# Set-attention and SwiGLU in one kernel: eight PSUM banks in one set, and one order for all steps behind the first gate product

## The chip, the cores and the metric

The kernel runs on one core of a Trainium2 chip, in one launch. The metric is the device time of one execution in microseconds (us). The engines are named as the profile names them: PE multiplies matrices (PEld is its weight load), DVE, ACT and POOL work element by element, and SP issues transfers. PSUM is the memory that PE writes its products to; it has eight banks, each of 128 x 512 numbers of four bytes.

## The reference

Four batches of 12416 tokens with 128 channels pass through attention with 32 inducing points, and then all 49664 tokens go through a normalised feed-forward part with 1536 inner columns.

```python
def mab(q, kv):
    s = scale * (q @ kv.transpose(0, 2, 1))
    s = s - s.max(-1, keepdims=True)
    a = np.exp(s)
    a /= a.sum(-1, keepdims=True) + 1e-09
    return a @ kv
h = mab(I, x)                  # 32 inducing points look at 12416 tokens
x = mab(x, h)                  # each token looks at the 32 points

rms = np.sqrt(np.mean(x * x, axis=-1, keepdims=True) + 1e-06)
xn = x / rms * rms_g
g = xn @ w_gate                # 128 -> 1536
silu = g * (1.0 / (1.0 + np.exp(-g)))
val = xn @ w_val               # 128 -> 1536
return (silu * val @ w_out).astype(np.float32)   # 1536 -> 128
```

## The kernel before

**Units and blocks.** A batch is cut into 25 units: 20 of 512 tokens, 4 of 480, and 1 of 256. The 1536 inner columns are cut into 12 groups of 128. A unit with one group is a block, so there are 100 units and 1200 blocks.

**One block.** PE makes the gate product (L682) from the unit's stacked attention weights, a tile `a` that holds an upper and a lower half, and a stacked factor matrix. ACT makes silu of it (L692); for a few blocks ACT makes tanh (L689) and DVE finishes the silu (L702). PE makes the value product (L710). DVE multiplies the two (L724, or L722 behind a tanh). The result must be multiplied by the 128 rows of w_out (`wo`) that belong to the block, and there are two ways to do it:

- A *plain* block (kind P) multiplies in full float32 (L781 from `wo`, two instructions, each of half the tokens).
- A *split* block cuts the result and the weights into upper and lower parts that PE multiplies at its faster fp32r setting. ACT makes the upper part (L737 for kind S, out of PSUM; L734 for kind D, out of a factor tile). For kind S DVE makes the lower part (L743); for kind D POOL does (L750), and ACT scales the upper part down (L756). Then PE makes two products (`project_two`, L769 and L770) into a bank `ups`, POOL adds the two parts (`add_in_place`, L789), and PE makes the third product (L781 too, from `xn` or `more`) into the bank `acc`.

**One unit.** When the products into `ups` are done, ACT takes them into an output tile (`take_upper`, step E, L822). When those into `acc` are done, DVE adds `acc` to it (`finish`, step F, L834) and transposes it (`turn_out`, step T, L842), and SP stores it with four transfers (`store`, step O, L855). SP also gathers the tile `a` of each unit (L592) and loads x for the next batch by channels (L147).

**Around it.** Attention for the next batch, its softmax, the normalisation, and the stacking of the factor matrices (`stack_of`, L504) run between the blocks of the batch before. In the first batch three more pieces do: the weights of gate and value arrive as raw words and are rounded in chunks (`rounding`: power, upper, sign, lower, with the last multiplication on POOL, L286; `put`, L228, writes the chunk back, and L216 fetches the next raw words), and `wo` is split into its upper, lower and difference parts (`split_wo`, L609 to L621, and `last_of`, L631 to L639).

**What sets the order.** The function `first` writes out the work up to the first gate product. The first 26 blocks, all plain, follow a plan written by hand (`early`: a block number with each side step, and a string `prefix` that places their plain products). From block 26 on, a string `program` gives the order: one letter is one step (`g` gate, `s` silu, `v` value, `m` the product of both, `h` upper part, `l` and `n` lower part, `e` scaling, `q` project_two, `d` add, `r` third product, `p` plain product, `E` `F` `T` `O` the steps of a unit, `a` a gather, and a dot for the next side step, whose number stands in `taken`). The string `sorts` gives the kind of each block; `banks`, `holders` and `workers` give the names of PSUM banks, factor tiles and work tiles that the steps use, one after the other. The engines run their own instructions in the order in which they were issued; a step waits for its operands and for its tile to come free.

**PSUM and tiles.** The eight banks are divided: five by name for gate and value products and the side work, `gv0` to `gv4`; two in rotation for `acc`; and one for `ups`, with these lines:

```python
ps_gv = pool("ps_gv", 1, space=PSUM)
ps_acc = pool("ps_acc", 2, space=PSUM)
ps_u = pool("ps_u", 1, space=PSUM)
...
def bank():
    ...
    return ps_gv.tile([P, 512], F32, name="gv", tag=f"gv{n}")
```

Output tiles are two in rotation. Factor tiles are `u0` to `u8` and ten places in three rings that hold other data at first.

Of the kernel before, what the change touches and what calls it, by code (L numbers as in the profile page):

```python
# [23 lines left out]
def kernel(  # L24
# [10 lines left out]

# [47 lines left out]
    outp = pool("outp", 2)  # L117
    ps_gv = pool("ps_gv", 1, space=PSUM)
    ps_acc = pool("ps_acc", 2, space=PSUM)
    ps_u = pool("ps_u", 1, space=PSUM)  # L120
# [66 lines left out]
    def warm(n):  # L187
        ps = ps_acc.tile([P, 512], F32, name="acc")
        for _ in range(n):
            nc.tensor.matmul(ps[:, 0:P], ident[:], ident[:], start=True, stop=True)  # L190

    warm(7)
    ps = ps_gv.tile([P, 512], F32, name="gv", tag="gv4")
# [25 lines left out]
    w0 = {}  # L219

    def rounding(i, c):
# [4 lines left out]
        def put():  # L226
            if i < 2:
                nc.sync.dma_start(out=w32[i][c][:], in_=st["dst"])  # L228
            if unread:
                fetch_raw(*unread.pop(0))  # L230
# [11 lines left out]
        def power():  # L242
            if i < 2:
                t = (xnp.tile([P, 512], F32, name=f"xn{2 * c - 1 + i}") if c else
                     silp.tile([P, 512], F32, name="silu") if i else halves.tile([P, 512], F32, name="lo"))
                w0[i, c] = t[:]
                dst = st["dst"] = w0[i, c]
            else:
                dst = st["dst"] = wo.rearrange("p j c -> p (j c)")[:, ts(c, 512)]
# [16 lines left out]
        def upper():  # L266
            if wide:
                f = st["f"] = outp.tile([P, 512], I32, name="o")
# [12 lines left out]
        def lower():  # L281
            if wide:
                e, f = st["e"], st["f"].bitcast(F32)
                nc.vector.scalar_tensor_tensor(out=f[:], in0=st["low"].bitcast(U32), scalar=2.0 ** -52, in1=f[:],
                                               op0=ALU.mult, op1=ALU.add)
                nc.gpsimd.tensor_tensor(out=st["dst"], in0=f[:], in1=e.bitcast(F32)[:], op=ALU.mult)  # L286
            put()
# [6 lines left out]
    NB, turn, turns, works, factors = 5, [0], [], [int(c) for c in "01201212"], []  # L294

    def bank():
# [5 lines left out]
        return ps_gv.tile([P, 512], F32, name="gv", tag=f"gv{n}")  # L302
# [5 lines left out]
    def attention(b, load_next):  # L308
# [192 lines left out]
        def stack_of(i, c):  # L501
# [3 lines left out]
            nc.scalar.copy(out=stacks[b][i][:, ts(c, 512)], in_=ps[:])  # L505
# [78 lines left out]
    def gather(b, u):  # L584
# [4 lines left out]
        a = moving[b, u] = (xnp.tile([P, 512], F32R, name="xn0") if (b, u) == (0, 2) else  # L589
# [4 lines left out]
    def split_wo(step):  # L594

        if not step:
            kws["first"] = xnp.tile([P, half + NK, C], F32R, name=f"xn{full - 1}")
            rings = [xnp.tile([P, RING * 512], F32R, name=f"xn{full - 4 + n}") for n in range(3)]
            kws["room"] = [ring[:, ts(n, 512)] for ring in rings for n in range(RING)][:3 * RING - 2]
            kws["wide"], kws["own"] = rings[2], {}  # L600

        def part(kind, g):
            n = kind * NK + g * half
            t = kws["first"][:, n:n + half, :] if n < half + NK else kws["more"][:, n - half - NK:n - NK, :]
            return t, t.bitcast(F32)

        def scaled(kind, g, mul, src=None):
            to, now = part(kind, g)
            nc.scalar.activation(to, now if src is None else src, AF.Copy, scale=mul)  # L609

        for g in range(2):
            one = wo[:, g * half:(g + 1) * half, :]
            at = step - g
            if at == 0:
                scaled(0, g, 1.0 - 2.0 ** -13, one)
            if at == 1:
                nc.gpsimd.tensor_tensor(out=part(1, g)[0], in0=one, in1=part(0, g)[1], op=ALU.subtract)
            if at == 3:
                scaled(1, g, 4096.0)
            if at == 4:  # L620
                nc.gpsimd.tensor_tensor(out=part(2, g)[0], in0=part(0, g)[1], in1=part(1, g)[1], op=ALU.subtract)  # L621
            if at == 6:
                scaled(0, g, -4096.0)

    def last_of(step):

        n = NJ - NK
        room = rings_last()
        one, (whi, wlo, ws) = wo[:, NK:NJ, :], (room[:, ts(kind, n), :] for kind in range(3))
# [11 lines left out]
    def rings_last():  # L641
        return kws["wide"][:, 2 * 512:4 * 512].rearrange("p (k c) -> p k c", c=C)

    def weight_of(kind, j):
        if j >= NK:
            return rings_last()[:, kind * (NJ - NK) + j - NK, :]
        n = kind * NK + j
        return kws["first"][:, n, :] if n < half + NK else kws["more"][:, n - half - NK, :]

    blocks, kinds = [], []  # L650
    at_unit = {}
    lists = {name: [] for name in "hlneqdDrRpx"}
# [3 lines left out]
    def unit_of(b, u):  # L656
        if (b, u) not in at_unit:
            s, q = units[u]
            at_unit[b, u] = {"T": per2[s] * m, "a": moving.pop((b, u)), "left": NJ, "q": 0, "acc": None,
                             "k": sum(kind != "P" for kind, one in zip(kinds, blocks) if one[:2] == (b, u)), "ups": None,  # L660
                             "o": None}
# [6 lines left out]
    def factor():  # L668
        return up.tile([P, 512], F32, name="u", tag=f"u{factors.pop(0)}")

    def room():
        n = factors.pop(0)
        if n < HELD and n not in kws["own"]:
            kws["own"][n] = up.tile([P, 512], F32R, name="u", tag=f"u{n}")[:]
        return kws["own"][n] if n < HELD else kws["room"][n - HELD]
# [36 lines left out]
    def times_value():  # L712
# [5 lines left out]
        else:  # L718
            factor_of[n] = {"u": factor()[:, 0:T]}
# [39 lines left out]
    def project_two():  # L759
# [5 lines left out]
        if one["ups"] is None:  # L765
# [724 lines left out]
```

## Time and profile before

| | |
|---|---|
| median of 3 runs | 1512.47 us (1512.46 to 1514.63) |
| profiled execution, span | 1513.0 us |
| first gate product | 47.3 us |
| last gate product | 1502.6 us |
| PE busy | 1496.2 us, 7138 matmuls |
| DVE busy | 1454.9 us, 2570 instructions |
| POOL busy | 1362.4 us, 1114 instructions |
| ACT busy | 1268.6 us, 2457 instructions |

The profile is of one execution, and its span is the time that the page gives for it; it lies 0.5 us above the median of the runs. Busy time of PE runs past the point at which the next matmul can start, so the distance between two starts tells more than the duration of a record. In the list of groups, a line of a helper stands for all its callers: L781 holds the plain products (out of `wo`) and the third products of split blocks (out of `xn` and `more`). In the blocks counted from the kernel, 384 are plain and 816 are split (657 of kind S, 159 of kind D).

### The profile page before, as it was taken

The numbers are of one execution on the slowest core, as the hardware profiler recorded it, in microseconds if no ns is written. First come the engines' busy times: TensorE is split into PE (matmuls) and PEld (weight loads), VectorE is DVE, ScalarE is ACT, GpSimd is POOL, SyncE is SP. The second block draws the span as 40 slices with busy tenths as digits, with TensorE's granted clock in tenths as the row PEclk, the third lists the DMA queues.
The fourth block names the chain that finished last, engine by engine and source line by source line (L and its number), as shares of the span: only waits on it lengthen the run. The fifth ranks groups of instructions, "written<-read, shape, count | busy, mean of one in ns | idle before, by whom it ended". The sixth has DMA issues, their size and how long they took to land.

```text
span 1513.0 us, 25789 instructions
## 1 busy us (share of the span) xinstructions
PE 1496.2 (99%) x7138; PEld 1090.8 (72%) x7138; DVE 1454.9 (96%) x2570; ACT 1268.6 (84%) x2457; POOL 1362.4 (90%) x1114
## 2 busy tenths in 40 slices
PE   9999999999999999999999999999999999999998
PEld 6547667766777767766777777776678777777787
DVE  6989999999999999989999999999999999999997
ACT  5778888878889889887988888887888988888886
POOL 1369998998989998999999999898889999999998
PEclk9999999999999999999999999999999999999999
DMA  7386226444352323554444233633212121221222
GB/s 285 93 136 118 39 36 127 116 89 78 64 101 37 74 56 71 108 119 74 84 70 74 44 68 63 145 78 66 45 34 43 36 35 36 42 43 29 42 41 34
DMA packets 389327, 112.55 MB, mean 74 GB/s; under 512 B 365088, under 2 KB 369728, under 8 KB 386624
## 3 DMA queue, kind: packets, MB, share of 16 engines
q1 hardware_dynamic: 388592, 110.83, 36.8%
q8 instruction: 57, 0.93, 0.3%
q14 instruction: 86, 0.70, 0.2%
q10 hardware_dynamic: 592, 0.08, 0.0%
HBM read 53.95 MB, written 27.00 MB: 54 GB/s over the span
## 4 chain that ended last, share of the span: by engine, by line
PE 96%; DVE 2%; ACT 1%; issue 1%; POOL 0%; DMA 0%; SPq 0%; ACTq 0%; POOLq 0%
PE acc L781 32%; PE gv L682 17%; PE gv L710 17%; PE u L769 11%; PE u L770 11%; PE gv L340 3%; PE gv L544 1%; PE gv L392 1%; PE gv L907 1%; PE gv L485 0%; PE acc L190 0%; PE gv L504 0%; DVE u L724 0%; DMA out_dram<-o 0%; POOL xn L286 0%
## 5 line engine op out<-in xcount | busy, mean ns | idle before, releaser
L692 ACT ACTIVATE silu<-gv 128x512 f32<-128x512 f32 (+2 forms) x1173 | 664.1, 590 | 132.9 <-PE gv L682 120.8
L789 POOL TENSOR_TENSOR u<-xn,u 128x512 fp32r<-128x512 f32 (+2 forms) x399 | 495.6, 1258 | 24.3 <-PE u L770 22.8
L710 PE MATMUL gv<-a,sv 128*128 128x512 f32 (+2 forms) x1188 | 472.5, 398 | 2.2 <-ACT silu L692 2.1
L682 PE MATMUL gv<-a,sg 128*128 128x512 f32 (+2 forms) x1188 | 472.9, 399 | 0.1
L789 POOL TENSOR_TENSOR xn<-xn,xn 128x512 fp32r<-128x512 f32 (+2 forms) x340 | 424.9, 1262 | 29.2 <-PE u L770 21.0
L724 DVE TENSOR_TENSOR gv<-silu,gv 128x512 f32<-128x512 f32 (+2 forms) x653 | 424.3, 674 | 10.8 <-PE gv L710 8.1
L737 ACT ACTIVATE xn<-gv 128x512 fp32r<-128x512 f32 (+2 forms) x656 | 383.4, 593 | 45.1 <-DVE gv L724 35.0
L781 PE MATMUL acc<-u,wo 128*128 128x512 f32 (+2 forms) x768 | 376.5, 576 | 0.0
L724 DVE TENSOR_TENSOR u<-silu,gv 128x512 f32<-128x512 f32 (+2 forms) x520 | 336.5, 657 | 13.3 <-PE gv L710 5.5
L769 PE MATMUL u<-xn,xn 128*128 128x512 f32 (+2 forms) x778 | 294.3, 379 | 0.0
L682 PEld LDWEIGHTS gv<-a,sg 128*128 128x128 f32 x1188 | 224.6, 189 | 90.2 <-issue 18.1
L710 PEld LDWEIGHTS gv<-a,sv 128*128 128x128 f32 x1188 | 224.4, 189 | 84.1 <-issue 18.9
L743 DVE SCALAR_TENSOR_TENSOR xn<-xn,gv 128x512 fp32r<-128x512 f32 (+2 forms) x333 | 218.7, 663 | 2.9 <-ACT xn L737 2.3
L743 DVE SCALAR_TENSOR_TENSOR u<-xn,gv 128x512 fp32r<-128x512 f32 (+2 forms) x323 | 211.9, 663 | 3.1 <-ACT xn L737 2.0
L781 PEld LDWEIGHTS acc<-u,wo 128*128 128x128 f32 x768 | 143.8, 190 | 28.5 <-issue 12.0
L769 PEld LDWEIGHTS u<-xn,xn 128*128 128x128 f32 x778 | 147.2, 189 | 20.1 <-issue 2.7
L781 PE MATMUL acc<-xn,more 128*128 128x512 f32 (+2 forms) x347 | 160.3, 464 | 0.0
L781 PE MATMUL acc<-u,more 128*128 128x512 f32 (+2 forms) x328 | 154.6, 475 | 0.0
L750 POOL TENSOR_TENSOR xn<-u,xn 128x512 fp32r<-128x512 f32 (+2 forms) x80 | 101.3, 1268 | 6.5 <-ACT xn L734 4.7
L734 ACT ACTIVATE xn<-u 128x512 fp32r<-128x512 f32 (+2 forms) x156 | 97.9, 628 | 9.4 <-DVE u L724 5.8
L756 ACT ACTIVATE xn<-xn 128x512 fp32r<-128x512 f32 (+2 forms) x156 | 97.9, 628 | 5.6 <-POOL u L750 3.5
L789 POOL TENSOR_TENSOR xn<-xn 128x512 fp32r<-128x512 f32 (+2 forms) x73 | 92.0, 1262 | 9.6 <-PE u L770 9.1
(213 smaller groups left out, 1840.3 us busy)
## 6 DMA issues: line engine op xcount, KB each, us to landing
out_dram<-o SPq DMA_DIRECT2D x320, 64.0 KB, 2.0
xT<-in_x_dram SPq DMA_DIRECT2D x60, 256.0 KB, 4.7
xn<-in_x_dram SPq DMA_DIRECT2D x60, 256.0 KB, 5.0
a<-hi SPq DMA_DIRECT2D x156, 64.0 KB, 2.0
a<-lo SPq DMA_DIRECT2D x156, 64.0 KB, 2.0
xn<-in_x_dram SPq DMA_DIRECT2D x5, 1024.0 KB, 9.4
xn<-w SPq DMA_DIRECT2D x18, 256.0 KB, 3.8
out_dram<-o SPq DMA_DIRECT2D x64, 60.0 KB, 2.0
```

What stands on the lines that cost most here:

```text
L682: nc.tensor.matmul(g[:, 0:T], stacks[b][0][:, ts(j, P)], halves_in_turn(one["a"][:, 0:T]), start=True, stop=True)
L692: nc.scalar.activation(sl[:, 0:T], gates.pop(n)[:, 0:T], AF.Silu)
L710: nc.tensor.matmul(v[:, 0:T], stacks[b][1][:, ts(j, P)], halves_in_turn(one["a"][:, 0:T]), start=True, stop=True)
L724: nc.vector.tensor_tensor(out=to, in0=sl[:, 0:T], in1=v[:, 0:T], op=ALU.mult)
L734: nc.scalar.activation(hi, t["u"], AF.Copy, scale=1.0 - 2.0 ** -13)
L737: nc.scalar.activation(hi, t["u"], AF.Copy, scale=-(1.0 - 2.0 ** -13) * 2.0 ** -12)
L743: nc.vector.scalar_tensor_tensor(out=t["lo"], in0=t["hi"].bitcast(F32), scalar=4096.0, in1=t["u"], op0=ALU.mult, op1=ALU.add)
L750: nc.gpsimd.tensor_tensor(out=t["lo"], in0=t["u"], in1=t["hi"].bitcast(F32), op=ALU.subtract)
L769: nc.tensor.matmul(ups, weight_of(0, j), halves_in_turn(t["hi"]), start=not one["q"], stop=False)
L770: nc.tensor.matmul(ups, weight_of(1, j), halves_in_turn(t["lo"]), start=False, stop=last)
L781: nc.tensor.matmul(to.rearrange("p (n h) -> p h n", h=2) if step2 else to, lhsT, rhs, start=one["left"] == NJ, stop=one["left"] == 1)
L789: nc.gpsimd.tensor_tensor(out=t["lo"], in0=t["hi"].bitcast(F32), in1=t["lo"].bitcast(F32), op=ALU.add)
```

## The change

- All eight banks come from one pool and are called by name, `b0` to `b7`: `ups`, `acc`, gate and value products, the warming products at the start and the sums of `first` all take the name that stands next in `banks`.
- Output tiles (`o0`, `o1`) and factor tiles are called by name too; `room` gives a factor tile to plain and split blocks alike.
- The hand-written plan `early` and the string `prefix` are gone. All steps behind the first gate product stand in one new `program`. The kinds of the blocks are new with it: 363 are plain and 837 are split (666 S, 171 D); 17 blocks instead of 27 use the tanh.
- The rounding of weights is cut into smaller steps (`sign`, `lower`, `join`, `put`), and `split_wo` works on five groups of columns (4, 4, 1, 1 and 2) that can be placed by themselves; `stack_of` and its copy are two steps.
- A unit without split blocks is transposed by `turn_out` straight out of `acc`. A second path of `scale_up`, for units without an `ups` bank of their own, is there, and no unit takes it, since `OWN` covers all units. `add_by_transfer`, which no block used, is gone.

```diff
-    outp = pool("outp", 2)
-    ps_gv = pool("ps_gv", 1, space=PSUM)
-    ps_acc = pool("ps_acc", 2, space=PSUM)
-    ps_u = pool("ps_u", 1, space=PSUM)
+    outp = pool("outp", 1)
+    psum = pool("psum", 1, space=PSUM)
...
-        return ps_gv.tile([P, 512], F32, name="gv", tag=f"gv{n}")
+        return psum.tile([P, 512], F32, name="gv", tag=f"b{n}")
+
+    def output(dtype):
+        return outp.tile([P, 512], dtype, name="o", tag=f"o{outs.pop(0)}")
...
+        def join():
+            if wide:
+                e, f = st["e"], st["f"].bitcast(F32)
                 nc.gpsimd.tensor_tensor(out=st["dst"], in0=f[:], in1=e.bitcast(F32)[:], op=ALU.mult)
-            put()
...
+        def stack_copy(i, c):
+            nc.scalar.copy(out=stacks[b][i][:, ts(c, 512)], in_=st["stack", i, c][:])
...
+    GROUPED = {"0": ("first", 0, 4, 0), "1": ("more", 0, 4, 4), "8": ("first", 12, 1, 8), "9": ("more", 12, 1, 9),
+               "a": ("last", 0, 2, 10)}
...
+    def split_wo(group, step):
...
+    def room(kind=F32R):
         n = factors.pop(0)
-        if n < HELD and n not in kws["own"]:
-            kws["own"][n] = up.tile([P, 512], F32R, name="u", tag=f"u{n}")[:]
-        return kws["own"][n] if n < HELD else kws["room"][n - HELD]
+        return up.tile([P, 512], kind, name="u", tag=f"u{n}") if n < HELD else kws[n]
...
-        if one["ups"] is None:
-            one["ups"] = ps_u.tile([P, 512], F32, name="u3")
-        ups = one["ups"][:, 0:T]
+        where = "ups" if one["own"] else "acc"
+        if one[where] is None:
+            one[where] = bank()
+        to = one[where][:, 0:T]
...
         if one["acc"] is None:
-            one["acc"] = ps_acc.tile([P, 512], F32, name="acc")
+            one["acc"] = bank()
...
-    kinds += ["P"] * EARLY + list("".join(sorts.split()))
+    kinds += list("".join(sorts.split()))
...
-    for k in range(EARLY):
-        groups = picks.pop(0)
...
-        gate()
-        silu()
-        products(1)
-        value()
-        times_value()
-        for n, (step, args) in enumerate(plan.get(k, [])):
-            products(n + 2)
-            step(*args)
```

## The prediction

> **What bounds the kernel.** I read the page first, its busy times and the chain that ended last.
>
> ```profile
> PE 1496.2 (99%) x7138; PEld 1090.8 (72%) x7138; DVE 1454.9 (96%) x2570; ACT 1268.6 (84%) x2457; POOL 1362.4 (90%) x1114
> ...
> PE 96%; DVE 2%; ACT 1%; issue 1%; POOL 0%; DMA 0%; SPq 0%; ACTq 0%; POOLq 0%
> ```
>
> PE carries the chain, but DVE and POOL are so full that work taken from one of them is not free on another. A share over the span hides stages, so next the windows. I number the gate products (L682) 0 to 1199 in the timeline; the first starts at 47.3 us, and the stretches used below end at gates 100 (182.9), 400 (554.9), 900 (1167.0) and at the end (1513.0).
>
> ```profile
> 47.30:122.50 75.20, 70.43 (x255) 40.08 (x256) 67.90 (x112) 53.73 (x97) 42.83 (x36) 0.98 0.67 121
> ...
> 182.90:432.90 250.00, 249.51 (x1235) 180.30 (x1234) 243.34 (x429) 211.99 (x411) 230.05 (x187) 1.00 0.44 84
> ...
> 554.90:1167.00 612.10, 611.00 (x2952) 444.75 (x2951) 594.44 (x1040) 522.99 (x1014) 572.68 (x464) 1.00 0.38 73
> 1167.00:1394.30 227.30, 227.30 (x954) 174.88 (x953) 224.46 (x378) 201.89 (x387) 223.06 (x178) 1.00 0.21 39
> ```
>
> Columns: length, busy PE, PEld, DVE, ACT, POOL, then granted clock. PE looks full, yet a record of a matmul runs into the next. What one costs is the distance between two starts, so the timeline:
>
> ```profile
> 700.20 0.38 PE L769 MATMUL u<-xn,xn 128*128 128x512 f32 x1
> 700.41 0.38 PE L770 MATMUL u<-u,xn 128*128 128x512 f32 x1
> 700.63 1.02 PE L781 MATMUL acc<-u,wo 128*128 128x512 f32 x2
> 701.09 0.78 PE L682 MATMUL gv<-a,sg 128*128 128x512 f32 x1
> 701.70 0.38 PE L710 MATMUL gv<-a,sv 128*128 128x512 f32 x1
> ```
>
> A 512-wide product takes 0.2155 us (700.20 to 700.41 to 700.63). From 700.63 to 701.70 lie one plain product with wo and one gate product, 1.07, so the plain one costs 0.86, and a split block's three cost 0.65. In the same way an add on POOL costs 1.24 (three in 3.75), a 512-wide DVE step 0.598, an ACT one 0.477:
>
> ```profile
> 1291.49 3.75 POOL L789 TENSOR_TENSOR u<-xn,u 128x512 fp32r<-128x512 f32 x3
> ```
>
> With these prices, and each other instruction at the distance that its own kind shows, I add up PE, DVE and POOL between gate numbers, in each kernel's order. Before, PE's sum behind gate 0 is 1415.9 of 1465.7 us. Its idle time is 49.8: 10.8, 11.8, 18.8 and 8.4 in the four stretches, mostly pieces under a microsecond ahead of gate, value and third products.
>
> **The change, part by part.** *Kinds of blocks.* Plain blocks fall from 384 to 363 (25 fewer at 512, 10 more at 480, 6 fewer at 256). PE: 25 x 0.2155 - 10 x 0.202 + 6 x 0.108 = 4.0 us saved. POOL: adds 31.0 - 11.7 + 4.1, and the kind that takes its low half on POOL (L750) is 13 times more frequent at 512 and once less at 256, 15.4: +39, with small steps +40. DVE: 12 low halves more at 512, 18 tanh products fewer, the 480s the other way round: -1.8. ACT: 25 high halves (11.9), 13 more to scale (6.8), two table loads (1.283 each), less the 480s: +19. ACT is busy 84%, and takes this beside the rest. POOL does not, in every stretch.
>
> *Order, by stretch (sum before to sum after).* Gates 0 to 100: PE 124.8 to 126.6, POOL 98.7 to 127.5, because the first 26 blocks are no longer all plain. Before took 135.6. One wait of it goes: unit 2's take-over (L822) waited for the store of unit 0, which stood behind twelve x loads (L147, 86.02 to 104.52) on SP.
>
> ```profile
> 110.49 0.60 ACT L822 ACTIVATE o<-u 128x512 f32<-128x512 f32 x1 [2.77 <-DMA out_dram<-o]
> ...
> 111.62 0.64 PE L710 MATMUL gv<-a,sv 128*128 128x512 f32 x1 [2.09 <-ACT silu L692]
> ```
>
> PE waited 2.09 us, and the clock fell behind it:
>
> ```profile
> 112.00:116.00 4.00, 4.00 (x10) 2.54 (x9) 2.60 (x4) 2.64 (x6) 1.27 (x1) 0.60 0.52 79
> ```
>
> At half clock for 3.4 us it lost another 1.7. In after the first store is issued at gate 27 and the third take-over at gate 46 (38 and 43 before), so 3.8 us of the 10.8 go. Late next is PE itself: at gate 21 its sum is 24.4 against DVE's 29.3, where before both had 25.5, since DVE now also rounds weights and makes low halves. That lag I charge in full, 4.6 us. Result 126.6 + 7.0 + 4.6 = 138.2, **+2.6**. Ends: lag hidden, 133.6 (-2.0); lag plus one half-clock window, 139.9 (+4.3).
>
> The Trainium skill, "TensorE: Matmul & The Clock Gate", section "HAM oscillation — how this bites in real kernels", says that PE is throttled again by idle gaps over about 3.4 us. By that rule the wait above would have cost no clock; the trace had the clock down after 2.09 us, so here the row decides. By the rule alone the removed wait would bring 2.1 instead of 3.8 us, the sum would be 1509.0, and the rival on the clock below would get no chance.
>
> SP: two x loads now stand ahead of the put of a rounded chunk and of the last raw weights (before issued at 51.42). At 1.78 us for each issue (7.10 for four in the timeline) they leave at 55.0 and land 6.7 later (the page's row for such a fetch), 61.7; DVE reads them not before 67.0. Hidden by 5 us; without that cover it would cost the excess over 5. The rounding's last multiply goes to POOL in a step of its own, with 0.135 us of fixed part each; it lies in POOL's sum. Splitting wo in five groups changes 10 POOL and 15 ACT pieces to 6 and 9, in the sums too. Factor tiles and output tiles by name are the same number of tiles: nothing.
>
> *Banks.* Eight of them before too, as five, two and one; now any of them can serve any product. PE's weight loads wait some 54 us in all for releases of gate and value banks, of which PE's own idle ahead of gate and value products is 9.9 + 8.0. What freedom takes off that is shown by no row: between 0 and 17.9. I take 3.8 in gates 100 to 400, where both other engines get lighter (DVE 360.7 to 354.3, POOL 343.9 to 330.1): PE 360.2 to 358.4, idle 11.8 to 8.0, 372.0 to 366.4, **-5.6** (ends -9.6 with idle 4.0, and -1.8 with all of it).
>
> Gates 400 to 900: PE 593.3 to 589.8, DVE 587.1 to 586.1, but POOL 570.2 to 593.7, now the largest. With PE's 18.8 kept, 608.6; POOL would then be at 97.5%. Before it ran at 93.2% over this stretch (570.2 of 612.1), but in the pieces where its sum was the largest (gates 650 to 700: 61.9 of 61.9 us; 1000 to 1050: 58.2 of 58.6) at 99% and over. I take 97.5%, 608.9, **-3.2**; ends 99%, 599.7 (-12.4), and 93.2%, 637.0 (+24.9).
>
> Gates 900 to the end: PE -0.5, DVE +6.3 (337.1, as PE): **+0.5** (ends -0.5, +3). The start, up to gate 0, keeps its PE sum of 34.0: 0.
>
> Sum: 2.6 - 5.6 - 3.2 + 0.5 = -5.7. From the profiled execution's 1513.0 that is 1507.3. The runs' median is 1512.47, 0.5 below the span; I leave that out.
>
> **Rivals.** *Slower: POOL becomes the bound in gates 400 to 900.* For it: 23.5 us more there on an engine whose waits are long ones, each for a project_two:
>
> ```profile
> POOL xn L789 <- PE u L770: 16.8, 18, 3.2
> ...
> POOL u L789 <- PE u L770: 7.8, 6, 3.3
> ```
>
> An add waits for L770, and PE's third product for the add; if POOL idles like that while it is the fullest, the time is not got back. Everything else as forecast, it decides at 614.6 us for the stretch, POOL at 96.6%. At 95% it is 625.0, +12.9 for the stretch and 16 more than the forecast's: 1523. Against it: the pieces at 99%. Chance 0.35.
>
> *Banks give more.* Half of the 17.9 us ahead of gate and value products goes besides: 1498. For it the 54 us of waiting loads; against it that most of those waits lie under a running product. 0.12.
>
> *No difference.* The banks were eight already, and with three engines within 30 us of each other the 4.0 us of PE come back as waits for POOL; only the store wait goes, and the lag replaces it: 1512. 0.12.
>
> *The clock.* The lag of 4.6 us comes in pieces of 2 us as at 111.62 and trips the half clock three times, 3 x 1.7 = 5.1: 1512.4. Against it: before had only one such window in the steady part. 0.03.
>
> **Numbers.** The forecast has 0.38, with 1500 to 1509 as its own range. 0.2% is 3 us, about what a measurement tells from no change: below 1509.5 lie the forecast and the banks, 0.50; within, no difference and clock, 0.15; above 1515.5 the slower rival, 0.35. The range goes down to 1495 (banks) and up to 1524, which leaves out the upper part of the POOL rival, some 0.13, and 0.04 below.
>
> **What would show it.** Right: gate 100 at about 185.5, gate 400 at 552, gate 900 at 1161; no wait of L822's successor for a store near 110; POOL at 97% or more from gate 400 to 900; PE's idle ahead of gates and values smaller. Wrong: POOL under 96.6% there with PE waiting for adds ahead of third products; a half clock before gate 50; a lag at gate 21 well off 4.6 us.

## The result, and the profile after

The kernel after takes 1549.06 us (median of 4 runs, 1547.55 to 1550.13) where before took 1513.13 beside it. The ratio is 1.0234 (95% interval 1.0219 to 1.0248): 35.9 us slower, outside the predicted range of 1495 to 1524. The profiled execution has a span of 1546.8 us, 33.8 more than before's.

The page of the kernel after, its busy times and the chain that ended last:

```profile
PE 1507.5 (97%) x7159; PEld 1102.8 (71%) x7159; DVE 1477.1 (95%) x2569; ACT 1290.1 (83%) x2500; POOL 1405.5 (91%) x1151
...
PE 89%; ACT 4%; DVE 3%; issue 2%; DMA 1%; POOL 0%; SPq 0%; ACTq 0%; DVEq 0%; POOLq 0%
```

PE's share of the chain fell from 96% to 89%, and POOL, which has 43 us more to do, is not on it. DVE is 22 us busier, although the change takes 1.8 us of work off it. That is the first sign: instructions of DVE got longer.

The windows of the kernel after, for the four stretches of the prediction (gates 0 to 100, to 400, to 900, and to the end; columns are length, busy PE, PEld, DVE, ACT, POOL, granted clock, share and rate of the DMA):

```profile
46.60:193.50 146.90, 137.12 (x528) 84.55 (x527) 133.78 (x215) 120.91 (x225) 130.05 (x106) 0.99 0.50 90
193.50:566.30 372.80, 371.54 (x1747) 266.66 (x1746) 359.62 (x631) 311.25 (x601) 333.55 (x271) 1.00 0.41 78
566.30:1200.80 634.50, 616.30 (x2977) 454.30 (x2976) 611.85 (x1044) 533.88 (x1039) 598.19 (x483) 0.99 0.37 72
1200.80:1546.80 346.00, 340.79 (x1457) 266.01 (x1455) 338.93 (x585) 297.90 (x581) 334.51 (x274) 1.00 0.21 38
```

Before took 135.6, 372.0, 612.1 and 346.0 us for them. So 11.3 us are lost at the start, 0.8 in the second stretch, 22.4 in the third and none in the last; the first gate product comes 0.7 earlier. In the third stretch nearly all of it lies at two places: gates 400 to 450 take 74.1 us (62.9 before), and gates 700 to 750 take 71.5 (65.6 before, with 5.2 us more PE work there in the old order).

At the first of the two places, DVE in the timeline of the kernel after (start, duration, engine, line, operation):

```profile
598.48 0.69 DVE L675 TENSOR_TENSOR gv<-silu,gv 128x512 f32<-128x512 f32 x1
599.08 8.93 DVE L329 TENSOR_TENSOR owns<-gmx,quarter 128x28 f32<-128x28 f32 x1
607.93 0.68 DVE L694 SCALAR_TENSOR_TENSOR xn<-xn,gv 128x512 fp32r<-128x512 f32 x1
```

A product of 128 x 28, a step of the softmax of the next batch (`max1`, once for each of batches 1 to 3), takes 8.93 us, thirteen times as long as one of 128 x 512 beside it. POOL in the same stretch:

```profile
598.09 2.55 POOL L743 TENSOR_TENSOR xn<-xn,xn 128x512 fp32r<-128x512 f32 x2
600.57 1.30 POOL L559 TENSOR_TENSOR lo<-aT,hi 128x512 fp32r<-128x512 f32 x1
601.79 4.96 POOL L743 TENSOR_TENSOR u<-u 128x512 fp32r<-128x512 f32 x4
606.66 1.30 POOL L743 TENSOR_TENSOR u<-xn,u 128x512 fp32r<-128x512 f32 x1
610.39 1.28 POOL L743 TENSOR_TENSOR xn<-xn,xn 128x512 fp32r<-128x512 f32 x1 [2.43 <-PE gv L722]
```

POOL works without a gap until 606.66 + 1.30 = 607.96, and then has nothing ready. The small product on DVE ends at 599.08 + 8.93 = 608.01, in that gap. Everything behind it on DVE stands, and so does PE:

```profile
600.23 0.38 PE L735 MATMUL gv<-xn,more 128*128 128x512 f32 x1
608.66 0.79 PE L633 MATMUL gv<-a,sg 128*128 128x512 f32 x1 [8.05 <-DVE xn L694]
609.25 0.63 PE L721 MATMUL gv<-xn,more 128*128 128x512 f32 x1
```

The products behind it take 0.63 instead of 0.38 us; the windows show why, in the column of the clock (0.50):

```profile
600.60:608.60 8.00, 0.01 (x1) 0.00 (x0) 8.00 (x3) 0.31 (x1) 7.36 (x7) 0.70 0.00 0
608.60:613.90 5.30, 5.24 (x13) 4.29 (x14) 4.59 (x9) 2.77 (x5) 2.54 (x2) 0.50 0.00 0
```

The same happens at 979.83: 8.22 us on DVE, until POOL falls idle at 988.00, and PE waits 6.95 us ahead of the product that needs `owns` (L334), again with half clock behind it. One line of each kernel tells the whole of it, in the answer for the source line of this step (duration in ns, minimum, median, maximum); first before, then after:

```profile
L352 DVE TENSOR_TENSOR owns<-gmx,quarter x3: 182/959/1660, 210.4 to 935.2; 128x28 f32<-128x28 f32 x3
```

```profile
L329 DVE TENSOR_TENSOR owns<-gmx,quarter x3: 883/8219/8931, 228.4 to 979.8; 128x28 f32<-128x28 f32 x3
```

At the start the same thing comes in small coin. DVE and then POOL of the kernel after, in the timeline:

```profile
72.69 1.50 DVE L227 TENSOR_SCALAR we<-sg 128x512 int32<-128x512 int32 x1
74.10 1.48 DVE L240 TENSOR_SCALAR o<-sg 128x512 int32<-128x512 int32 x1
```

```profile
72.63 1.27 POOL L701 TENSOR_TENSOR xn<-u,xn 128x512 fp32r<-128x512 f32 x1
73.86 2.86 POOL L743 TENSOR_TENSOR xn<-xn 128x512 fp32r<-128x512 f32 x2
```

Two steps of the weight rounding, 0.42 us each when POOL is quiet, end some 0.3 us behind the end of a POOL instruction (the first at 72.69 + 1.50 = 74.19, behind 72.63 + 1.27 = 73.90), as if they were held to that end and did the rest of their work then. Counted over the steps of rounding behind gate 0, by what each record lies above the shortest of its form (those of 0.25 us and more), DVE is held 7.8 us there; before it was 1.7, since the old plan had plain blocks at the start and POOL was busy 42.8 of the first 75 us, against 61.3 now.

### The profile page after: what moved, and what is told of

Read it like the earlier page. It is cut to its first block, busy times and chain, and to the rows that moved or that the text cites. A ratio compares the mean times of both kernels' runs of the same rounds, so it can differ in the third digit from the quotient of the medians.

```text
span 1546.8 us, 25751 instructions
## 1 busy us (share of the span) xinstructions
PE 1507.5 (97%) x7159; PEld 1102.8 (71%) x7159; DVE 1477.1 (95%) x2569; ACT 1290.1 (83%) x2500; POOL 1405.5 (91%) x1151
## 4 chain that ended last, share of the span: by engine, by line
PE 89%; ACT 4%; DVE 3%; issue 2%; DMA 1%; POOL 0%; SPq 0%; ACTq 0%; DVEq 0%; POOLq 0%
PE gv L735 29%; PE gv L633 16%; PE gv L661 16%; PE gv L721 11%; PE gv L722 11%; PE gv L317 3%; PE gv L523 1%; PE gv L369 1%; ACT silu L643 1%; PE gv L847 1%; ACT xn L688 0%; DVE gv L675 0%; DMA xn<-in_x_dram 0%; ACT sc L450 0%; DVE xn L694 0%
## 5 line engine op out<-in xcount | busy, mean ns | idle before, releaser
L743 POOL TENSOR_TENSOR xn<-xn,xn 128x512 fp32r<-128x512 f32 (+2 forms) x405 | 503.7, 1259 | 36.0 <-PE gv L722 32.5
L675 DVE TENSOR_TENSOR gv<-silu,gv 128x512 f32<-128x512 f32 (+2 forms) x660 | 434.7, 669 | 9.3 <-PE gv L661 5.1
L735 PE MATMUL gv<-u,wo 128*128 128x512 f32 (+2 forms) x726 | 360.8, 579 | 2.4 <-DVE u L675 2.4
L675 DVE TENSOR_TENSOR u<-silu,gv 128x512 f32<-128x512 f32 (+2 forms) x523 | 339.2, 659 | 22.0 <-PE gv L661 12.5
L694 DVE SCALAR_TENSOR_TENSOR xn<-xn,gv 128x512 fp32r<-128x512 f32 (+2 forms) x482 | 315.4, 659 | 8.7 <-ACT xn L688 6.3
L743 POOL TENSOR_TENSOR xn<-xn 128x512 fp32r<-128x512 f32 (+2 forms) x210 | 265.6, 1271 | 21.2 <-PE gv L722 16.4
L743 POOL TENSOR_TENSOR u<-xn,u 128x512 fp32r<-128x512 f32 (+2 forms) x160 | 199.1, 1254 | 5.5 <-PE gv L722 4.8
L701 POOL TENSOR_TENSOR xn<-u,xn 128x512 fp32r<-128x512 f32 (+1 forms) x133 | 169.7, 1278 | 18.6 <-ACT xn L685 14.9
L721 PE MATMUL gv<-xn,xn 128*128 128x512 f32 (+2 forms) x415 | 162.9, 393 | 0.2
L735 PEld LDWEIGHTS gv<-u,wo 128*128 128x128 f32 x726 | 134.9, 190 | 23.0 <-issue 4.8
L735 PE MATMUL gv<-xn,xn 128*128 128x512 f32 (+2 forms) x313 | 144.5, 462 | 0.8 <-POOL xn L743 0.7
L721 PE MATMUL gv<-xn,more 128*128 128x512 f32 (+2 forms) x343 | 132.8, 387 | 0.1
L735 PE MATMUL gv<-xn,more 128*128 128x512 f32 (+2 forms) x288 | 131.2, 456 | 0.0
L722 PE MATMUL gv<-xn,xn 128*128 128x512 f32 (+2 forms) x313 | 117.4, 375 | 1.4 <-DVE xn L694 1.4
L722 PE MATMUL gv<-xn,more 128*128 128x512 f32 (+2 forms) x288 | 108.8, 378 | 0.0
L685 ACT ACTIVATE xn<-u 128x512 fp32r<-128x512 f32 (+1 forms) x160 | 101.1, 634 | 5.2 <-DVE u L675 4.6
```

Source lines behind the costliest of these rows:

```text
L675: nc.vector.tensor_tensor(out=to, in0=sl[:, 0:T], in1=v[:, 0:T], op=ALU.mult)
L685: nc.scalar.activation(hi, t["u"], AF.Copy, scale=1.0 - 2.0 ** -13)
L694: nc.vector.scalar_tensor_tensor(out=t["lo"], in0=t["hi"].bitcast(F32), scalar=4096.0, in1=t["u"], op0=ALU.mult, op1=ALU.add)
L701: nc.gpsimd.tensor_tensor(out=t["lo"], in0=t["u"], in1=t["hi"].bitcast(F32), op=ALU.subtract)
L721: nc.tensor.matmul(to, weight_of(0, j), halves_in_turn(t["hi"]), start=not one["q"], stop=False)
L722: nc.tensor.matmul(to, weight_of(1, j), halves_in_turn(t["lo"]), start=False, stop=last)
```

## The experiments

The theory was this: **the door.** A DVE instruction that reads two operands from SBUF cannot go on beside a POOL instruction; it waits for the end of one, and sometimes for the end of all that POOL has ready. The rivals were that POOL is simply the bound (the slower rival of the prediction), that the instruction itself is slow, and that the order alone makes DVE and PE late. Before was run beside each group of runs (medians 1512.95 to 1515.21), so kernels of different groups are compared by their ratios to it.

### max1 on ACT

```diff
-            nc.vector.tensor_tensor(out=t[:], in0=st["gmx"][:].unsqueeze(1).to_broadcast((P, R, NS)),
-                                    in1=quarter[:].unsqueeze(2).to_broadcast((P, R, NS)), op=ALU.mult)
+            for q in range(R):
+                nc.scalar.activation(t[:, q, :], st["gmx"][:], AF.Copy, scale=quarter[:, q:q + 1])
```

> The kernel after, with the small step max1 (owns = gmx x quarter, 128 x 28, once for each of batches 1 to 3) made by four small ACT copies with a scale instead of one DVE product of two SBUF operands. Theory D (the door): a DVE instruction that reads two operands from SBUF cannot go on while POOL works through a queue of ready work; it is held until POOL runs dry, and PE stands behind it. Then the 8.9 and 8.2 us records are gone, PE's stalls of 8.2 and 7.1 us with the half clock behind the first go too, and since gates 400 to 450 and 700 to 750 lose 12.4 and 11.1 us beyond PE's own work, the time falls from 1549 by about 23 to 1526 (1522 to 1532). Theory P (POOL is simply the bound): POOL's work is the same, so the time stays at 1549 within 3 us and other waits take the place. Theory I (the instruction itself is slow, by its broadcast operands or the accumulated gmx): 1526 too; the probes tell it from D.

Measured: 1530.02 us, ratio 1.0103 (1.0088 to 1.0119). Three small instructions, two of them held for long, cost 19 us. Gates 400 to 450 fall from 74.1 to 64.4 us, 700 to 750 from 71.5 to 62.8. POOL's work is the same, so the theory that POOL is the bound is out as the cause of these two losses. The gain of 23 that was expected is 4 too large: the two stretches gave 18.4 back.

### POOL's queue shortened, max1 left where it was

```diff
+    def apart(n):
+        return 405 <= n < 428 or 702 <= n < 724
...
-        nc.gpsimd.tensor_tensor(out=t["lo"], in0=t["hi"].bitcast(F32), in1=t["lo"].bitcast(F32), op=ALU.add)
+        if not apart(n):
+            nc.gpsimd.tensor_tensor(out=t["lo"], in0=t["hi"].bitcast(F32), in1=t["lo"].bitcast(F32), op=ALU.add)
...
+        if apart(n):
+            nc.tensor.matmul(one["acc"][:, 0:one["T"]], weight_of(2, j), halves_in_turn(factor_of[n]["hi"]),
+                             start=one["left"] == NJ, stop=False)
```

> The kernel after, with max1 left on DVE, but POOL's queue ahead of it shortened: for the split blocks among 405 to 427 and 702 to 723 (18 and 17 blocks) POOL's add is left out, and PE makes the third product in two parts, of the upper and of the lower factor, with the same sum. PE gets 35 x 0.2155 = 7.5 us more. Theory D: POOL has no backlog when max1 comes, its records fall from 8.9 and 8.2 to 2 us or less, and the time to about 1549 - 23 + 7 = 1533 (1528 to 1539). Theory I: the records stay at 8 us or more, the time rises to 1553 to 1557. Theory P: POOL loses 43 us of work, and the time falls by up to 10 with no change of the max1 records beyond chance.

Measured: 1535.75 us, ratio 1.0141 (1.0126 to 1.0157). The answer for the source line of `max1`:

```profile
L329 DVE TENSOR_TENSOR owns<-gmx,quarter x3: 168/179/880, 228.5 to 974.2; 128x28 f32<-128x28 f32 x3
```

The same instruction with the same operands takes 0.17 and 0.18 us once POOL has no backlog. So it is not slow by itself, and what held it is POOL's queue.

### Sixty extra DVE instructions in the kernel before, in three forms

One is issued at every tenth gate product from 400 to 990; the three kernels differ in its form alone.

```diff
+        if name == "g" and 400 <= done["g"] < 1000 and done["g"] % 10 == 0:
+            probe()
...
+        # first form: two operands from SBUF
+        nc.vector.tensor_tensor(out=ident[:, 0:28], in0=fold[:, 0, 0:28], in1=fold[:, 1, 0:28], op=ALU.mult)
+        # second form: a minimum over one operand
+        nc.vector.tensor_reduce(out=ident[:, 0:1], in_=fold[:, 0, 0:28], axis=AX.X, op=ALU.min)
+        # third form: one operand and a constant number
+        nc.vector.tensor_scalar(out=ident[:, 0:28], in0=fold[:, 0, 0:28], scalar1=2.0, scalar2=None, op0=ALU.mult)
```

> The kernel before, with 60 extra DVE products of 128 x 28 (two constant SBUF operands, into a tile that nothing reads by then), one at every tenth gate product from 400 to 990. Theory D: each lasts until POOL has no ready work: the three of this kind in before took 0.18, 0.96 and 1.66 us, so 0.3 to 3 us each, mean about 1, the longest several us, 60 us in all, and the kernel gets 25 to 60 us slower (1537 to 1573). Theory I and theory P: 0.15 to 0.2 us each, 60 x 0.15 = 9 us of DVE, and the kernel is 2 to 9 us slower.

> The same as the run with 60 extra products, but each extra DVE instruction is a minimum over 128 x 28 of one SBUF operand. Theory D: with one operand read nothing is held, 0.1 to 0.2 us each, the kernel 2 to 9 us slower than before (1515 to 1522). Theories I and P expect the same here; a general delay of any DVE instruction that is not fed by PSUM would show as long records here too.

> The kernel before with 60 extra DVE instructions at the same places as the two probes, each a product of one SBUF operand of 128 x 28 with a constant number. In the kernel after, steps of the rounding with one SBUF operand, which take 0.42 us for 512 elements where most DVE steps take 0.65, were held too (1.50 and 1.48 us). Theory D2 (this fast form needs the same door as two operands): 0.4 to 1 us each on average, the kernel 20 to 45 us slower (1535 to 1560). Theory D1 (only the second operand counts): 0.1 to 0.2 us each, the kernel up to 5 us slower (1513 to 1519).

Measured: 1558.41 us with two operands, ratio 1.0302 (1.0273 to 1.0331); 1516.31 with the minimum, ratio 1.0008 (0.9998 to 1.0018); 1559.63 with one operand and a number, ratio 1.0307 (1.0289 to 1.0326). The answers for the source line of each, in this order:

```profile
L1451 DVE TENSOR_TENSOR ident<-fold x60: 141/712/4111, 553.8 to 1310.4; 128x28 f32<-128x28 f32 x60
```

```profile
L1451 DVE TENSOR_REDUCE ident<-fold x60: 135/170/176, 555.5 to 1270.1; 128x1 f32<-128x28 f32 x60
```

```profile
L1451 DVE TENSOR_SCALAR ident<-fold x60: 134/702/4108, 555.3 to 1312.1; 128x28 f32<-128x28 f32 x60
```

An instruction of 0.14 us costs 0.7 in the middle case and 4.1 in the worst; the minimum never costs more than 0.18. The second operand is not what matters: the product with a number has one operand and is held just as long. The minimum also writes one column and not 28; but the transposes of x, which read and write whole tiles in SBUF, are not held either (0.66 to 0.71 us in the kernel after), so writing to SBUF is not enough. In both held forms 43 of the 60 lie 0.25 us or more above the shortest, 43.0 us in all, and the kernel is some 43 to 46 us slower: a microsecond of DVE held is about a microsecond of the kernel there, although DVE is not the longest.

### max1 on ACT in the kernel before

The edit is the first one, on before.

> The kernel before, with max1 made by four small ACT copies for batches 1 to 3, as in the first run on the kernel after. Theory D: its three DVE records (0.18, 0.96, 1.66 us) and PE's stall of 1.26 ahead of max2 go: 1 to 3 us faster, about 1511 to 1513 where before is 1513 to 1515. A rival: the stalls there are hidden, and four more ACT steps change nothing: within 1 us.

Measured: 1514.93 us, ratio 0.9999 (0.9991 to 1.0008). No gain: a hold of 1.66 us is covered there, and the expected 1 to 3 us are a miss. This is also the version that might have beaten both kernels, and does not.

### POOL emptied at the start, and filled again

With `max1` on ACT in all three. The first kernel takes 24 of POOL's steps at the start away; the second and third put idle POOL work of 3 x 0.45 and of 1 x 1.24 us in the place of each step that was replaced.

```diff
+        return n < 26                      # apart(n), as above
...
         if step == 1:
-            nc.gpsimd.tensor_tensor(out=wlo, in0=one, in1=whi.bitcast(F32), op=ALU.subtract)
+            if n == 4:
+                nc.scalar.activation(wlo, whi.bitcast(F32), AF.Copy, scale=2.0 ** -12)
+                fill()                     # second and third kernel
+            else:
+                nc.gpsimd.tensor_tensor(out=wlo, in0=one, in1=whi.bitcast(F32), op=ALU.subtract)
...
+        if n < 26:                         # low_of_u
+            nc.scalar.activation(t["lo"], t["u"], AF.Copy, scale=2.0 ** -12)
+            fill()
```

> The kernel after with max1 on ACT, and with POOL's work at the start taken away: the differences of the first two groups of wo (split_wo) and the lower parts of kind D among the first 26 blocks are replaced by scaled ACT copies (other numbers than the reference's), and the adds of the first 26 blocks are left out (third product in two parts, PE +15 x 0.2155 = 3.2 us). POOL keeps the last multiplications of the rounding. Theory D: the DVE steps of the rounding were held by POOL for 7.8 us there in all; without that they take 0.4 to 0.8 us each, and gates 0 to 100, 148 us with max1 on ACT, come down to 140 to 143 (time 1522 to 1525). Theory O (the order alone makes DVE late, 4.6 us as charged): the records shorten, but gates 0 to 100 stay at 146 to 150, and the time at 1528 to 1533.

> As the run with POOL's work at the start taken away, but for each POOL step that was replaced POOL makes three products of 128 x 128 of constants in SBUF (about 0.45 us each, nobody waits for them). Dependences, DVE, ACT and PE are those of that run; only POOL is as full as before. Theory D: the DVE steps of the rounding are held again, and gates 0 to 100 take 146 to 150 us, 5 to 8 more than in that run. Theory O: no difference beyond 1 us, since nothing waits for these products.

> As the run with POOL's work at the start taken away, but for each POOL step that was replaced POOL makes one product of 128 x 512 of constants into a spare place (about 1.24 us, as long as the step that it stands for; nobody waits for it). With three fillers of 0.45 us each gates 0 to 100 took 144.7 us, against 143.2 with none and 148.3 with the real steps. Theory D, made sharper (a DVE step is held to the end of the POOL instruction that runs, so the length of one instruction counts, not POOL's share of busy time): the rounding's records are held by 4 us or more in all, and gates 0 to 100 take 146 to 149. If it is the dependence on POOL's results that costs and not the hold: 143 to 145.

Measured, time and ratio, then from the trace gates 0 to 100, the microseconds by which the rounding was held (counted as above), and those at half clock in this stretch:

| | time, us | ratio to before | gates 0 to 100 | held | half clock |
|---|---|---|---|---|---|
| max1 on ACT alone | 1530.02 | 1.0103 (1.0088 to 1.0119) | 148.3 | 7.8 | 10.2 |
| POOL emptied | 1526.49 | 1.0073 (1.0058 to 1.0089) | 143.2 | 0.5 | 0 |
| filled with 3 x 0.45 us | 1528.22 | 1.0084 (1.0070 to 1.0098) | 144.7 | 2.0 | 3.4 |
| filled with 1 x 1.24 us | 1530.51 | 1.0109 (1.0093 to 1.0125) | 147.0 | 5.6 | 6.8 |

The groups by line and form show the same step in the kernel with max1 on ACT, with POOL emptied, and filled with long steps (busy us, mean ns, idle before):

```profile
L240 DVE TENSOR_SCALAR o<-sg 128x512 int32<-128x512 int32 x2 | 1.9, 952 | 0.0
```

```profile
L240 DVE TENSOR_SCALAR o<-sg 128x512 int32<-128x512 int32 x2 | 0.9, 442 | 0.0
```

```profile
L242 DVE TENSOR_SCALAR o<-sg 128x512 int32<-128x512 int32 x2 | 1.7, 852 | 0.0
```

The emptied kernel lies just above its expectation (143.2 against 140 to 143 us). The short fillers missed theirs by far (1.5 us instead of 5 to 8), and that miss sharpened the theory: the hold lasts to the end of the POOL instruction that runs, so three short ones hold DVE less than one long one of the same busy time. With long fillers, for which nobody waits, 3.8 of the 5.1 us come back. So at the start it is mostly the hold that costs, not a dependence on POOL's results: between 46 and 195 us PE's waits for DVE grow from 3.0 us with POOL emptied to 6.5 with long fillers, while those of PE's weight loads for POOL fall from 7.0 to 5.3. With POOL emptied PE had 3.2 us more to do, so 143.2 understates the gain.

The half clock is a rival, since its time grows with the holds, and each figure for gates 0 to 100 is from one execution. But the runs' times do not hang on it: among executions with the same mean granted clock, 0.998, the emptied kernel took 1526.85 us, the one with short fillers 1528.08 and 1528.32, and the one with long fillers 1530.50.

### Less POOL, less ACT, less DVE behind gate 100

With `max1` on ACT, gates 100 to 1199 still take 1325.5 us against 1319.7 in before, although PE's sum there is 5.8 us smaller. Each cut below takes work off one engine, in both kernels but for the first.

```diff
+        return n >= 100 and n % 36 == 7 and kinds[n] != "P"          # apart(n), as above
```

> The kernel after with max1 on ACT (1530), and with the third product in two parts for 26 split blocks spread from block 100 to the end: PE +26 x 0.2155 = 5.6 us, POOL 26 adds less, -32 us. It asks what still makes the part behind gate 100 slower than in before (1325.5 us to the last gate against 1319.7) although PE's sum is 5.8 us smaller. Theory P (POOL, the fullest there, sets the pace): 0 to 8 us faster, 1522 to 1530. Theory N (PE's small waits come from the order of steps and banks, not from POOL's load): 3 to 6 us slower, 1533 to 1536.

```diff
-        nc.scalar.activation(t["hi"], t["hi"].bitcast(F32), AF.Copy, scale=-(2.0 ** -12))
+        if n < 100:
+            nc.scalar.activation(t["hi"], t["hi"].bitcast(F32), AF.Copy, scale=-(2.0 ** -12))
```

> The kernel after with max1 on ACT (1530), and without ACT's scaling of the upper part in the 143 blocks of kind D from block 100 on (other numbers than the reference's): ACT 143 x 0.52 = 74 us less. It asks whether the small waits of PE behind gate 100 come from ACT, which has 19 us more to do in the kernel after; PE's waits for silu ahead of value products are 16.4 us there against 10.4 in before. Theory A (ACT is late): 4 to 10 us faster, 1520 to 1526. Theory N (the order): within 2 us of 1530.

> The same edit on the kernel before: no scaling in the 142 blocks of kind D from block 100 on, ACT 74 us less. Theory A: ACT is not late there, within 2 us of before; then a gain in the run on the kernel after is what ACT costs the new order. If before gains as much, ACT's lateness is in both and explains no difference.

```diff
-        nc.gpsimd.tensor_tensor(out=t["lo"], in0=t["hi"].bitcast(F32), in1=t["lo"].bitcast(F32), op=ALU.add)
+        if n < 100 or n % 4:
+            nc.gpsimd.tensor_tensor(out=t["lo"], in0=t["hi"].bitcast(F32), in1=t["lo"].bitcast(F32), op=ALU.add)
```

> The kernel after with max1 on ACT (1530), and without POOL's add in every fourth block from block 100 on where it is split (201 adds, 249 us of POOL; the third product takes the lower part alone, other numbers than the reference's). PE, DVE and ACT have the same work. Theory P2 (POOL's lateness makes PE's extra waits in the new order): 8 us or more faster, to 1522 or below, and more than the same cut gives in before. Theory N (the order of PE's own steps): the same gain as in before, within 2 us.

> The same cut in the kernel before (192 adds). Theory P2: 0 to 5 us faster. Theory N: as much as in the kernel after.

```diff
-                nc.vector.transpose(out=t[:, ts(k, n * m)], in_=t[:, ts(k, n * m)])
                 return
```

> The kernel after with max1 on ACT (1530), and without DVE's transposes of x for batches 1 to 3 (84 steps, about 46 us of DVE; other numbers than the reference's). Theory V (DVE's lateness makes PE's extra waits): 8 us or more faster, more than the same cut gives in before. Theory N: the same gain as in before, within 2 us.

> The same cut in the kernel before. Theory V: 0 to 5 us faster. Theory N: as much as in the kernel after.

| cut | after with max1 on ACT: ratio | gates 100 to 1199 | before: ratio | gates 100 to 1199 |
|---|---|---|---|---|
| none | 1.0103 (1.0088 to 1.0119) | 1325.5 | 1 | 1319.7 |
| 26 adds for 5.6 us of PE | 1.0125 (1.0112 to 1.0139) | 1329.3 | | |
| ACT, 62 and 57 us | 1.0093 (1.0079 to 1.0107) | 1323.6 | 0.9997 (0.9988 to 1.0005) | 1318.9 |
| POOL, 235 and 224 us | 1.0107 (1.0092 to 1.0123) | 1324.7 | 0.9987 (0.9977 to 0.9996) | 1317.3 |
| DVE, 36 and 34 us | 1.0111 (1.0096 to 1.0126) | 1324.8 | 1.0005 (0.9995 to 1.0014) | 1319.8 |

The microseconds of ACT, POOL and DVE are the differences of the busy times on the pages, in after and in before; the expectations name more (74, 249, 238 and 46), counted by price. None of the cuts brings the gain of 4 to 8 us and more that would have made its engine the cause.

The windows for gates 400 to 900, first with max1 on ACT, then with the cut of POOL besides:

```profile
567.60:1183.50 615.90, 611.76 (x2977) 450.83 (x2976) 594.90 (x1042) 535.30 (x1047) 597.86 (x483) 1.00 0.38 74
```

```profile
567.00:1182.30 615.30, 611.63 (x2977) 452.14 (x2977) 593.96 (x1042) 535.03 (x1047) 496.37 (x398) 1.00 0.38 75
```

A hundred microseconds less on POOL in this stretch (597.86 to 496.37) shorten it by 0.6. So POOL was not what set the pace there, full as it looked, nor is DVE. ACT accounts for about 1 to 2 us. The one cut with a price, 5.6 us more on PE, made the part 3.8 us longer: PE's own work does count.

What is left stands in PE's order itself, as far as the traces tell. The work that PE does between a block's gate product and its value product is 1.32 us on average in the kernel after and 1.75 in before (sum of the prices over PE's order, blocks 100 on), and PE's idle time ahead of value products, between 183 and 1500 us, is 11.9 us with max1 on ACT and 4.9 in before. It stays at about 11 with the cuts of ACT and of POOL. By this reading the value product there comes too soon behind the gate product for ACT and DVE to have done their part. This was read, not tried: no run moved the value products back, so the cause of this part is not shown.

## Why the prediction was wrong, point by point

**The prices.** It priced each DVE step by its kind and width, as if a step cost the same beside any other engine. That is the step that failed. The term that was missing is the time for which POOL holds DVE. At two of the `max1` of the kernel after DVE is held 16.8 us (8.93 and 8.22, against 0.17 and 0.18 with POOL's queue shortened); PE waits 15.0 us there (8.05 and 6.95) and loses more at the half clock behind, and without them the time is 19 us shorter. In the rounding DVE is held 6 us more than before. That makes some 25 of the 39.5 us by which the profiled span missed the forecast (1546.8 against 1507.3). Most of the rest lies behind gate 100, 6.4 us to gate 400 and 7.0 to gate 900, and its cause stays open. The signs stood in the profile of before, in rows that the prediction did not use: 0.18, 0.96 and 1.66 us for three equal instructions, and 1.32 us for one step of the rounding (L278 at 49.30) where the others took 0.7. No rival had it either. The Trainium skill, "GPSIMD Engine Reference", section 1 "Specifications", says that GpSimd's way to SBUF is shared with VectorE, with contention for DVE instructions that have two SBUF inputs or run in a mode that uses two ports. The runs agree, with 0.7 us in the middle case and 8.9 in the worst for an instruction of 0.14 to 0.18; the page gives no size.

**Gates 0 to 100.** Forecast 138.2, measured 146.9. The store wait went as the prediction said: PE shows no wait over 0.8 us from 81 us to the first `max1`. But 1.7 of the 3.8 us taken off for it were half clock, and that was chance (below, on the clock). The lag was charged too small. At gate 21 the kernel after is 39.8 us behind its first gate product and before 31.4, although PE's sum is 1.1 us smaller there, so the lag grew by 9.5 us and not by 4.6; that is one of the signs of being wrong that the prediction named. With POOL emptied it grew by 4.6 (34.9 us at gate 21), some of that from this run's extra products. So the charge about covers what the new order does by itself, and the rest is the hold, with the half clock at gate 3. The whole stretch says the same: 143.2 us with POOL emptied, of which 3.2 are extra PE work, so 140.0 against 138.2. Single traces differ here by up to 3 us: 133.0 to 135.9 in seven traces with before's start, 146.8 to 148.3 in six with that of after.

**Gates 100 to 400.** Forecast 366.4, measured 372.8. The 3.8 us for the freedom of banks did not come; PE's idle rose from 11.8 to 14.4 instead of falling to 8.0. It was the one term that no row showed, and it should not have entered the sum with a sign.

**Gates 400 to 900.** Forecast 608.9, measured 634.5, of which 18.6 go with `max1` on ACT. The remaining 615.9 lie 7 above the forecast. There POOL, by the prediction's own sum, is at 593.7 of 615.9, 96.4% (the trace has 597.86 busy), just under the 96.6% at which the slower rival was to decide; and yet that rival was wrong in its mechanism, since the cut of POOL changed nothing. That the time came out on its side is no merit of it: its price was 16 us, and the cause another.

**Gates 900 to the end.** Forecast +0.5, measured 0.0.

**The clock.** Its rival was given three small pieces of half clock. The kernel after has one at the start, from 50.78 to 54.20 us, at gate 3, behind a wait of PE of 2.36 us; a half clock before gate 50 was another sign of being wrong. It has two more behind the held `max1`: PE works 5.3 us at half clock behind the first and 4.2 behind the second, and about half of that, 4.7 us, is lost. With `max1` on ACT the start is the same, and its trace has 10.2 us of half clock there, three times as much; the stretch took 148.3 us instead of 146.9, so two pieces more cost 1.4 and not 3.4.

What the prediction saw in before was right for that row and no rule. In the kernel before with `max1` on ACT, which changes nothing up to that place, PE waits as long and the clock stays full (the timeline, then the window that the prediction showed of before):

```profile
111.43 0.48 PE L710 MATMUL gv<-a,sv 128*128 128x512 f32 x1 [2.22 <-ACT silu L692]
```

```profile
112.00:116.00 4.00, 4.00 (x17) 2.96 (x16) 4.00 (x7) 3.90 (x9) 2.47 (x2) 1.00 0.57 86
```

Of six traces that have this wait, three (1.92 to 2.22 us) keep the full clock and take 133.8 to 134.0 us for gates 0 to 100, and three (2.09 to 2.48 us) fall to half and take 135.6 to 135.9. So the prediction took off 1.7 us that before loses in some executions only. The rule that it set against the trace, from the Trainium skill, "TensorE: Matmul & The Clock Gate", section "HAM oscillation — how this bites in real kernels", agrees with the waits of 8.05 and 6.95 us, which are over 3.4; it does not account for the half clock behind 2.09 and 2.36.

**PE's saving of 4.0 us.** The price per product is borne out in part, as 5.6 us more on PE cost 3.8; but the new order lost more in waits than it saved in products.

## What to carry to other kernels

Before moving a step beside a full POOL, look whether it is a DVE instruction that reads two operands from SBUF, or a fast one with a single operand (0.42 us for 512 columns here, where most steps take 0.65 to 0.7): its cost is then not its own duration alone but also what is left of POOL's instruction, or of all that POOL has ready, and all of DVE stands behind it. On ACT the four copies in place of one such step took 0.3 us each and were not held, and DVE was not held with an operand in PSUM or in a plain reduction. The sign in a profile is one group whose minimum and maximum lie far apart. And an engine that is 97% busy is not the bound for that reason alone: take work off it and see.

## What the runs showed of the hardware that was not expected

- In the run with 60 products of two SBUF operands all 43 held records end 40 to 48 ns behind the end of a POOL instruction. Most end with the POOL instruction that ran when they began; six ran on to the end of the second to fourth, up to 4.11 us, and in the kernel after two ran to the end of the seventh and the eighth, until POOL had nothing ready. The held steps of the rounding, with 512 columns, end 0.28 to 0.65 us behind such an end. What decides between the two cases is open: POOL had its next instruction ready in many of the short cases too.
- POOL is not slowed while it holds DVE: its adds beside the record of 8.93 us take 1.22 to 1.25 us from start to start, as elsewhere. Where a fast DVE step was already running, POOL's instruction is the longer one (1.51 us at 67.32, where 1.27 is usual).
- One kind of POOL instruction holds nothing: inside the root on 128 x 16 (L560, 2.9 us) three probes with two operands took 0.14 to 0.18 us. Whether its few elements or its operation makes the difference is not shown.
- DVE steps with one operand in PSUM show none of it: the steps L675 and L694, which are most of DVE's work, take 0.64 to 0.70 us in all their 1488 records at 512 columns in the kernel after. Nor do the transposes of x, with one operand in SBUF (0.66 to 0.71 us at 512 and 480 columns).
